# A transformer block's backward pass on one core: another order of work behind the attention

## Chip, core, metric

The kernel runs on one core of a Trainium2 chip, as one program of some 51,000 instructions. The metric is the device time of one execution, in microseconds (us), as the median of several runs. The engines named below are TensorE (PE, matrix products and transposes; PEld is its loading of weights), VectorE (DVE), ScalarE (ACT), GpSimd (POOL) and SyncE (SP, which here only issues DMA transfers). Each engine takes its own instructions in program order and waits for other engines by semaphores. On-chip tiles lie in SBUF; matrix products are summed in banks of PSUM.

## What is computed

The forward value of one block and all gradients of it, for a sequence of 2048 with D = 512, 32 heads of 16 and a hidden width F of 1792, in bfloat16:

```python
xn = layernorm(x)
s  = softmax_attention(xn @ wqkv) @ wo               # A_ref
y  = layernorm(xn)
h  = gelu_tanh(y @ w1 + b1)
g  = silu(h @ w2 + b2)                               # silu of B_ref
out = x + s * g
out, vjp = jax.vjp(f, x, wqkv, wo, w1, b1, w2, b2)
return out, *vjp(grad_out)    # outputs 0..7: out, dx, dwqkv, dwo, dw1, db1, dw2, db2
```

## The kernel before

It has three parts that run one after the other. The first (`phase_pre`, from line 42) computes the projections, the MLP's forward part and the gates, and puts into DRAM what the last part needs: `H1T_s` (the MLP's pre-activation, transposed), `HGT_s` (its gelu, transposed), `GB_s` (per row the gate g and grad_out times a gate factor), `DSO_s` (the gradient at the attention's output projection), `Y_s` (y). The second (`attention_core`, line 822) runs forward and backward of the attention for 16 pairs of heads, with PE, ACT and DVE in orders that are written out by hand. It leaves the attention's output O in the SBUF tile `Oall` and the gradients of q, k and v in `dQall` and DRAM (`dKVT_s`). The diff touches neither.

The third part, `phase3` (line 498), is the post-attention part. The sequence is cut into NT = 16 tiles of 128 rows, D into IC = 4 blocks, F into FC = 14 blocks; `FG` groups the 14 blocks by 4, 4, 4 and 2. PSUM is split into four banks for products over 512 rows or columns (`psA`), two for transposes (`psT`), two for the weight gradients (`psW`). In order:

- Output stage (L556 to L611). For each of 16 row tiles: O is transposed by PE (`o_turn`, `o_tp`, copied by ACT to `oTt`), multiplied with wo (`ps_so`, L595, four matmuls). DVE multiplies the product with one gate to `dm_all` (the gradient dm at the MLP's output) and with the other to `t1`; POOL adds x to `t1` into `ot`, which is stored every fourth tile as out_0 (issued by POOL). `dm_turn` transposes dm into `dmT`. The gates come as `gb4`, 1 MB for four row tiles, by SP (`load4`); w2 comes transposed by a DMA (`w2T`).
- db2 and dwo (L614 to L631): column sums of dm by 16 matmuls with a vector of ones (`psdb2`), then four tiles `ps_dwo` of 16 matmuls from O and `ds4`, each copied by ACT and stored.
- dw2 (L632 to L645): 14 tiles `ps_dw2` of 16 matmuls, from `hgc` (gelu, turned by DMA: one set of four transposes by SP for two tiles) and `dm_all`.
- dh1 and dw1 (L648 to L688). For each of the 14 blocks of F, 4 x 4 matmuls `ps_dhg` of w2T and dmT; DVE multiplies the product with gelu' into `dh1T`, where gelu' lay, and sums it for db1. A DMA transposes each block into `dhc`. When a group of FG is done, the four tiles `ps_dw1` of the group before follow (16 matmuls each, of `y_all` and `dhc`), copied by ACT to one of two buffers `dw1` and stored by POOL. The last group has two blocks, so its matmuls have 256 columns. w1 is loaded transposed (`w1T`) after the second group.
- dy (`ps_dy`, L719), with the backward of the second layer norm on ACT and DVE, then dx, dwq and dwkv. Unchanged.

gelu' is computed between these: `gelu_grad` (L533) does one of 28 pieces (two blocks of F by 512 rows, tiles of 128x1024). It loads `h1` by SP; then ACT Square, DVE L542 and L543 (`w`), ACT Identity and two Sigmoids (the second of the negative), and four steps on DVE (L549 to L552), the last of which writes into dh1T. Two pieces are called in the output stage (after row tiles 11 and 15), one with each dwo tile, one with each dw2 tile, and the rest before the dh1 blocks of the later groups.

The order on each engine in this part is set by the tile scheduler, which emits instructions by the waits it foresees; the program's order is a preference only. Within `tc.manual_schedule(engines=...)` the named engines keep the program's order. Where two tiles share a place in SBUF, the later one waits for the last use of the earlier one. The pools take places from the left or right side of SBUF in the order in which they are opened, and give them back when closed.

Of the kernel before, what the change touches and what calls it, by code (L numbers as in the profile page):

```python
# [8 lines left out]
bf16 = mybir.dt.bfloat16  # L9
f32 = mybir.dt.float32  # L10
# [487 lines left out]
def phase3(ctx, tc, k, A_x, A_wqkv, A_wo, B_w1, B_w2, grad_out, out_0, out_1, out_2, out_3, out_4, out_5, out_6, out_7, dbg):  # L498
# [14 lines left out]
    with ExitStack() as c1:  # L513
# [12 lines left out]
        with ExitStack() as cL:  # L526
# [6 lines left out]

            def gelu_grad(j, g):

                cs = slice(g * 512, (g + 1) * 512)
                h1 = ew.tile([128, 2, 512], bf16, name="h1", bufs=3)
                nc.sync.dma_start(out=h1[:], in_=k.H1T_s[j, g])
                sq = ew.tile([128, 2, 512], bf16, name="sq")
                nc.scalar.activation(out=sq[:], in_=h1[:], func=ACT.Square, scale=float(np.sqrt(2.0 * GC * GA)))  # L540
                w = ew.tile([128, 2, 512], bf16, name="w", bufs=1)
                nc.vector.tensor_scalar(out=w[:], in0=sq[:], scalar1=2.0 * GC, scalar2=None, op0=ALU.add)  # L542
                nc.vector.tensor_tensor(out=w[:], in0=w[:], in1=h1[:], op=ALU.mult)  # L543
                nc.scalar.activation(out=sq[:], in_=sq[:], func=ACT.Identity, scale=3.0, bias=c2gc[:])
                sg = ew.tile([128, 2, 512], bf16, name="sg")
                nc.scalar.activation(out=sg[:], in_=w[:], func=ACT.Sigmoid)
                sp = ew.tile([128, 2, 512], bf16, name="sp")
                nc.scalar.activation(out=sp[:], in_=w[:], func=ACT.Sigmoid, scale=-1.0)
                nc.vector.tensor_tensor(out=sp[:], in0=sp[:], in1=h1[:], op=ALU.mult)  # L549
                nc.vector.tensor_tensor(out=sp[:], in0=sp[:], in1=sq[:], op=ALU.mult)  # L550
                nc.vector.tensor_scalar(out=sp[:], in0=sp[:], scalar1=1.0, scalar2=None, op0=ALU.add)
                nc.vector.tensor_tensor(out=dh1T[:, 2 * j:2 * j + 2, cs], in0=sp[:], in1=sg[:], op=ALU.mult)  # L552
            gel = [(j, g) for j in range(FC // 2) for g in range(4)]

            cM = cL.enter_context(ExitStack())
            dmp = pool(cM, "p3_dm", side="right")  # L556
            dm_all = dmp.tile([128, NT, D], bf16, name="dm_all")
            with ExitStack() as c2:
# [21 lines left out]
                nc.sync.dma_start_transpose(out=w2T[:], in_=B_w2)  # L580
                o_turn(0)
                o_turn(1)

                def dm_turn(t):
# [3 lines left out]
                    nc.scalar.copy(out=dmT[:, :, t * 128:(t + 1) * 128], in_=pt[:])  # L588
                for t in range(NT):
                    if t % 4 == 1 and t + 4 < NT:  # L590
                        load4(t // 4 + 1)
                    ps = psA.tile([128, D], f32, name="ps_so", tag="mm")
                    o = oTt.pop(t)
                    for cc in range(IC):
                        nc.tensor.matmul(ps[:], lhsT=o[:, cc, :], rhs=wo_sb[:, cc, :], start=(cc == 0), stop=(cc == IC - 1))  # L595
                    gb = gb4[t // 4]
                    nc.vector.tensor_tensor(out=dm_all[:, t, :], in0=ps[:], in1=gb[:, t % 4, 1, :], op=ALU.mult)
                    t1 = b2.tile([128, D], f32, name="t13")
                    nc.vector.tensor_tensor(out=t1[:], in0=ps[:], in1=gb[:, t % 4, 0, :], op=ALU.mult)
                    if t % 4 == 0:  # L600
                        ot = b2.tile([128, 4, D], bf16, name="ot3")
                    nc.gpsimd.tensor_tensor(out=ot[:, t % 4, :], in0=t1[:], in1=x4[t // 4][:, t % 4, :], op=ALU.add)
                    if t % 4 == 3:
                        nc.gpsimd.dma_start(out=rows4(o0, t // 4), in_=ot[:])
                    if t + 2 < NT:
                        o_turn(t + 2)
                    if t >= 1:
                        dm_turn(t - 1)
                    if t in (11, 15):
                        gelu_grad(*gel.pop(0))  # L610
                dm_turn(NT - 1)  # L611
            with ExitStack() as c2:
                b2 = pool(c2, "p3a_dw2", 2, side="right")
                ds4 = [b2.tile([128, 4, D], bf16, name="ds4", bufs=4) for q4 in range(4)]  # L614
# [8 lines left out]
                for ac in range(IC):  # L623
# [7 lines left out]
                    gelu_grad(*gel.pop(0))  # L631
                for fc in range(FC):  # L632
                    if fc % 2 == 0:
                        hgc = b2.tile([128, 4, 2, 4, 128], bf16, name="hgc")
                        for g in range(4):
                            nc.sync.dma_start_transpose(out=hgc[:, g].rearrange("p l t f -> p (l t) f"),
                                                        in_=k.HGT_s[fc // 2, g].rearrange("p l c -> p (l c)"))
                    ps = psW.tile([128, D], f32, name="ps_dw2", tag="w")
                    for t in range(NT):
                        nc.tensor.matmul(ps[:], lhsT=hgc[:, t // 4, fc % 2, t % 4, :], rhs=dm_all[:, t, :], start=(t == 0), stop=(t == NT - 1))  # L640
                    dw2 = b2.tile([128, D], bf16, name="dw2")
                    nc.scalar.copy(out=dw2[:], in_=ps[:])
                    nc.gpsimd.dma_start(out=out_6[fc * 128:(fc + 1) * 128, :], in_=dw2[:])
                    gelu_grad(*gel.pop(0))
            cM.close()  # L645
            w1T = pool(cL, "p3_w1").tile([128, FC, D], bf16, name="w1T")
            with ExitStack() as c2:
                b2 = pool(c2, "p3b", 2, side="right")  # L648
                y_all = b2.tile([128, NT, D], bf16, name="y_all", bufs=1)
                nc.sync.dma_start(out=y_all[:].rearrange("p (g t) d -> p g t d", g=4), in_=k.Y_s.rearrange("g p t d -> p g t d"))  # L650
                dhc = {}

                def do_dw1(gi):
                    f0, nf = FG[gi]
                    fn = nf * 128
                    for ic in range(IC):
                        ps = psW.tile([128, 512], f32, name="ps_dw1", tag="w")
                        for t in range(NT):
                            nc.tensor.matmul(ps[:, 0:fn], lhsT=y_all[:, t, ic * 128:(ic + 1) * 128], rhs=dhc[gi][:, t, 0:fn],
                                             start=(t == 0), stop=(t == NT - 1))  # L660
                        dw1 = b2.tile([128, 512], bf16, name="dw1")
                        nc.scalar.copy(out=dw1[:, 0:fn], in_=ps[:, 0:fn])
                        nc.gpsimd.dma_start(out=out_4[ic * 128:(ic + 1) * 128, f0 * 128:f0 * 128 + fn], in_=dw1[:, 0:fn])
                for gi, (f0, nf) in enumerate(FG):
                    dhc[gi] = b2.tile([128, NT, 512], bf16, name="dhc")
                    for fl in range(nf):
                        fc = f0 + fl
                        if gi and gel:
                            gelu_grad(*gel.pop(0))
# [17 lines left out]
                nc.vector.tensor_copy(out=db1[:], in_=db1f[:])  # L687
                nc.sync.dma_start(out=out_5.rearrange("(c p) -> p c", p=128), in_=db1[:])  # L688
            cW.close()

# [613 lines left out]
```

## Time and profile before

| | us |
|---|---|
| median of 3 runs (2321.96 to 2326.19) | 2322.59 |
| profiled execution, of which the span of its instructions | 2325.73, 2324.0 |
| PE busy in the span (96%) | 2228.9 |
| ACT busy (88%) | 2046.3 |
| DVE busy (87%) | 2021.2 |
| POOL busy (15%) | 341.9 |

The columns of the next table are the stretch of the span in us, its length, busy us of PE and of DVE, and the clock that PE was granted as a share of full speed.

| stretch | what runs on PE | length | PE | DVE | clock |
|---|---|---|---|---|---|
| 0 to 155 | first part | 155.0 | 129.98 | 102.39 | 0.97 |
| 155 to 1959 | attention | 1804.0 | 1771.60 | 1697.72 | 1.00 |
| 1959 to 1965 | start of the third part | 6.0 | 1.31 | 3.77 | 0.87 |
| 1965 to 2000.5 | output stage, first dh1 matmuls | 35.5 | 32.15 | 30.64 | 0.97 |
| 2000.5 to 2015.8 | dwo | 15.3 | 14.05 | 10.92 | 1.00 |
| 2015.8 to 2073 | dw2 | 57.2 | 50.85 | 32.67 | 0.97 |
| 2073 to 2098.5 | dh1 | 25.5 | 18.15 | 22.07 | 0.89 |
| 2098.5 to 2171.3 | dh1 and dw1 | 72.8 | 72.35 | 46.71 | 0.99 |
| 2171.3 to 2187.9 | the last of dw1 | 16.6 | 7.72 | 0.00 | 0.69 |
| 2187.9 to 2324 | dy, dx, dwqkv | 136.1 | 130.68 | 74.31 | 0.99 |

Where PE is busy for less than the length of a row, it waits for something there.

### The profile page before, as it was taken

The page shows a single profiled execution, that of the slowest core. Times are in us where ns is not written, and L with a number is a line of the kernel's source. Part 1 is how long each engine was busy: PE and PEld are TensorE (multiplying, and loading weights), DVE is VectorE, ACT ScalarE, POOL GpSimd, SP SyncE. Part 2 cuts the span into 40 slices and gives each one's busy share as a digit, 9 for nine tenths or more (in the row PEclk, how much of TensorE's full clock was granted, in tenths as well). Part 3 has the DMA queues.
Part 4 walks back from the last instruction along what each step waited for, and adds up shares of the span by engine and source line. Part 5 has one row for each costly group of instructions (what it writes and reads, how often), then busy time and mean ns, then how long its engine had stood idle before and what let it go on. Part 6 is the DMA issues. An engine that isn't in the chain of part 4 may idle for free.

```text
span 2324.0 us, 50898 instructions
## 1 busy us (share of the span) xinstructions
PE 2228.9 (96%) x20082; PEld 796.1 (34%) x20128; DVE 2021.2 (87%) x3593; ACT 2046.3 (88%) x2337; POOL 341.9 (15%) x804
## 2 busy tenths in 40 slices
PE   7898999999999999999999999999999998889899
PEld 3342333333333333333333333333333333434444
DVE  6577899999999999999999999999999996767255
ACT  6566999999999999999999999999999999786133
POOL 4330111111111111111111111111111111310000
PEclk9999999999999999999999999999999999999999
DMA  9787999999998999999999999999999898996961
GB/s 287 229 279 176 169 174 169 179 163 184 161 186 163 180 167 179 165 179 168 175 175 167 180 164 186 163 184 162 181 167 179 155 160 195 241 212 138 169 181 65
DMA packets 1310113, 415.56 MB, mean 179 GB/s; under 512 B 1272273, under 2 KB 1285073, under 8 KB 1308721
## 3 DMA queue, kind: packets, MB, share of 16 engines
q1 hardware_dynamic: 1303984, 395.92, 90.3%
q0 software_dynamic: 4304, 12.98, 1.7%
q10 hardware_dynamic: 1584, 3.41, 0.4%
q8 instruction: 157, 2.57, 0.4%
q14 instruction: 84, 0.68, 0.1%
HBM read 46.52 MB, written 49.03 MB: 41 GB/s over the span
## 4 chain that ended last, share of the span: by engine, by line
PE 77%; issue 8%; DVE 8%; DMA 3%; ACT 2%; POOL 1%; SPq 1%; ACTq 0%; POOLq 0%; DVEq 0%
PE d L933 12%; PE X L970 11%; PE s L911 11%; PE Z L1051 9%; PE X L983 7%; PE Z L1043 5%; DVE gts L950 5%; PE t L923 5%; PE ET L895 5%; PE ps_dy L719 2%; PE XT L995 2%; PE X L973 1%; PE ps_dwkv L752 1%; PE ps_dxa L771 1%; DMA out_dram<-dw 1%
## 5 line engine op out<-in xcount | busy, mean ns | idle before, releaser
L950 DVE TENSOR_TENSOR gts<-d,et 128x512 bf16<-128x512 f32 x2048 | 1321.8, 684 | 73.8 <-PE d L933 23.0
L939 ACT ACTIVATE et<-s 128x1024 bf16<-128x1024 f32 x1024 | 1043.0, 1044 | 8.9 <-PE d L933 8.2
L944 ACT ACTIVATE e<-t 128x1024 bf16<-128x1024 f32 x832 | 866.2, 1042 | 25.2 <-PE t L923 5.4
L933 PE MATMUL d<-QDT,KVT 32*128 32x512 bf16 x2048 | 757.2, 384 | 18.2 <-DVE gts L950 16.9
L911 PE MATMUL s<-QDT,KVT 32*128 32x512 bf16 x2048 | 398.5, 385 | 5.0 <-ACT et L939 2.9
L1051 PE MATMUL Z<-gk,W 128*32 128x512 bf16 x2048 | 397.5, 385 | 0.0
L970 PE MATMUL X<-et,Lc 128*32 128x512 bf16 x2048 | 369.8, 389 | 0.0
L973 PE MATMUL X<-et,NAT 128*32 128x512 bf16 x2048 | 368.7, 388 | 0.0
L983 PE MATMUL X<-gts,NAT 128*17 128x512 bf16 x2048 | 330.4, 381 | 0.0
L1043 PE MATMUL Z<-e,W 128*32 128x512 bf16 x1664 | 321.8, 383 | 3.9 <-POOL W L1022 1.6
L923 PE MATMUL t<-KVT,QDT 32*128 32x512 bf16 x1664 | 323.6, 384 | 1.0 <-ACT e L944 1.0
L933 PEld LDWEIGHTS <-KVT 32*128 32x128 bf16 x2048 | 173.1, 91 | 234.8 <-issue 234.4
L911 PEld LDWEIGHTS <-KVT 32*128 32x128 bf16 x2048 | 106.1, 91 | 250.0 <-issue 230.3
L1017 POOL TENSOR_TENSOR W<-NATQd,rL 128x128 bf16<-128x128 bf16 x64 | 25.8, 403 | 1124.2 <-DVE rL L1016 1124.1
L1051 PEld LDWEIGHTS <-W 128*32 128x32 bf16 x2048 | 100.3, 95 | 172.9 <-issue 142.8
L923 PEld LDWEIGHTS <-QDT 32*128 32x128 bf16 x1664 | 92.3, 91 | 145.8 <-issue 141.0
L1043 PEld LDWEIGHTS <-W 128*32 128x32 bf16 x2048 | 105.0, 94 | 107.4 <-issue 96.7
L970 PEld LDWEIGHTS <-Lc 128*32 128x32 bf16 x2048 | 83.5, 93 | 162.2 <-issue 162.1
L900 DVE COPY eE<-ET 128x1024 bf16<-128x1024 bf16 x192 | 130.2, 678 | 4.4 <-PE ET L895 4.4
L895 PE MATMUL ET<-ident_bf,et 128*128 128x128 bf16 x1536 | 119.2, 220 | 2.1 <-DVE e L286 2.1
L895 PEld LDWEIGHTS <-et 128*128 128x128 bf16 x1536 | 86.5, 98 | 45.8 <-issue 45.8
L983 PEld LDWEIGHTS <-NAT 128*17 128x17 bf16 x2048 | 79.5, 89 | 59.4 <-issue 42.8
(203 smaller groups left out, 2354.1 us busy)
## 6 DMA issues: line engine op xcount, KB each, us to landing
gk<-gts SPq DMA_TRANSPOSE x512, 4.5
H1T_s<-h1p SPq DMA_DIRECT2D x28, 256.0 KB, 4.3
h<-H1T_s SPq DMA_DIRECT2D x28, 256.0 KB, 3.6
HGT_s<-hgT SPq DMA_DIRECT2D x21, 256.0 KB, 4.3
NAT_s<-NS SPq DMA_DIRECT2D x4, 1056.0 KB, 5.4
dKVT_s<-ob SPq DMA_DIRECT2D x16, 256.0 KB, 3.7
gb<-GB_s SPq DMA_DIRECT2D x4, 1024.0 KB, 6.8
Rkv<-dKVT_s SPq DMA_DIRECT2D x2, 2048.0 KB, 9.4
```

Source lines behind the costliest of these rows:

```text
L895: nc.tensor.transpose(ET[:, hj, m * 128:(m + 1) * 128], st_et[g - 3 + m][:, hj, 384:512], ident_bf[:])
L911: nc.tensor.matmul(s[:, hj, :], lhsT=op["KVT"][r, kb * 128:(kb + 1) * 128], rhs=op["QDT"][r, qc * 512:(qc + 1) * 512], start=True, stop=Tr ...
L923: nc.tensor.matmul(t[:, hj, :], lhsT=op["QDT"][r, q0:q0 + 128], rhs=op["KVT"][r, kc * 512:(kc + 1) * 512], start=True, stop=True, tile_pos ...
L933: nc.tensor.matmul(d[:], lhsT=op["KVT"][r, kb * 128:(kb + 1) * 128], rhs=op["QDT"][r, qc * 512:(qc + 1) * 512], start=True, stop=True, til ...
L939: nc.scalar.activation(out=et[:], in_=st_s.pop(g)[:], func=ACT.Exp)
L944: nc.scalar.activation(out=e[:], in_=st_t.pop(g)[:], func=ACT.Exp)
L950: nc.vector.tensor_tensor(out=gts[:, g % 2, hj], in0=st_d.pop((g, hj))[:], in1=st_et[g][:, hj], op=ALU.mult)
L970: nc.tensor.matmul(X[64 + 32 * hj:96 + 32 * hj, :], lhsT=Lc[:, :], rhs=et[:, hj, :], start=(kb == 0), stop=False, skip_group_check=True, t ...
L973: nc.tensor.matmul(X[32 * hj:32 * hj + 32, :], lhsT=NATt[:, kb, hj, 1:33], rhs=et[:, hj, :], start=(kb == 0), stop=(kb == 15), tile_positi ...
L983: nc.tensor.matmul(X[64 + 32 * hj:64 + 32 * hj + 17, :], lhsT=NATt[:, kb, hj, 0:17], rhs=gts[:, kb % 2, hj, :], start=False, stop=(kb == 1 ...
L1043: nc.tensor.matmul(Z[32 * hj:32 * hj + 32, :], lhsT=blk[j]["W1"][:, qb, hj, :], rhs=e[:, hj, :], start=(qb == 0), stop=False, tile_positio ...
L1051: nc.tensor.matmul(cur["Z"][32 * hj:32 * hj + 32, :], lhsT=blk[j]["W2"][:, qb, hj, :], rhs=grhs, start=False, stop=(qb == 3), tile_positio ...
```

## The change

All of it lies in `phase3`. gelu' is cut into three functions: `gelu_a` (load, Square, two DVE steps), `gelu_b` (Identity and the two Sigmoids, the one of the negative now first) and `gelu_c` (four DVE steps). The output stage keeps the program's order on PE, ACT and DVE; three pieces of gelu' are laid into it by these parts, where two whole ones were before. `t13` has three buffers for two. `dm_all` moves to the left side. The dw2 tile becomes a function; tiles 0 to 9 come as before, tiles 10 to 13 each before one of the first four dh1 blocks, and each of these four blocks now takes a piece of gelu' as well. `y_all` takes O's place (`Oall`) in place of a tile of its own. The pool of w1T is opened after the first dh1 group, and the odd `dhc` go to a pool of their own on the left. `dw1` has eight buffers for two.

```diff
--- before.py
+++ after.py
@@ -531,9 +531,10 @@
             cW = cL.enter_context(ExitStack())
             ew = pool(cW, "p3_ew", 2, side="right")
 
-            def gelu_grad(j, g):
-
-                cs = slice(g * 512, (g + 1) * 512)
+            gu = {}
+
+            def gelu_a(j, g):
+
                 h1 = ew.tile([128, 2, 512], bf16, name="h1", bufs=3)
                 nc.sync.dma_start(out=h1[:], in_=k.H1T_s[j, g])
                 sq = ew.tile([128, 2, 512], bf16, name="sq")
@@ -541,19 +542,32 @@
                 w = ew.tile([128, 2, 512], bf16, name="w", bufs=1)
                 nc.vector.tensor_scalar(out=w[:], in0=sq[:], scalar1=2.0 * GC, scalar2=None, op0=ALU.add)
                 nc.vector.tensor_tensor(out=w[:], in0=w[:], in1=h1[:], op=ALU.mult)
+                gu[j, g] = h1, sq, w
+
+            def gelu_b(j, g):
+                h1, sq, w = gu[j, g]
                 nc.scalar.activation(out=sq[:], in_=sq[:], func=ACT.Identity, scale=3.0, bias=c2gc[:])
                 sg = ew.tile([128, 2, 512], bf16, name="sg")
-                nc.scalar.activation(out=sg[:], in_=w[:], func=ACT.Sigmoid)
                 sp = ew.tile([128, 2, 512], bf16, name="sp")
                 nc.scalar.activation(out=sp[:], in_=w[:], func=ACT.Sigmoid, scale=-1.0)
+                nc.scalar.activation(out=sg[:], in_=w[:], func=ACT.Sigmoid)
+                gu[j, g] = h1, sq, sg, sp
+
+            def gelu_c(j, g):
+                h1, sq, sg, sp = gu.pop((j, g))
                 nc.vector.tensor_tensor(out=sp[:], in0=sp[:], in1=h1[:], op=ALU.mult)
                 nc.vector.tensor_tensor(out=sp[:], in0=sp[:], in1=sq[:], op=ALU.mult)
                 nc.vector.tensor_scalar(out=sp[:], in0=sp[:], scalar1=1.0, scalar2=None, op0=ALU.add)
-                nc.vector.tensor_tensor(out=dh1T[:, 2 * j:2 * j + 2, cs], in0=sp[:], in1=sg[:], op=ALU.mult)
+                nc.vector.tensor_tensor(out=dh1T[:, 2 * j:2 * j + 2, g * 512:(g + 1) * 512], in0=sp[:], in1=sg[:], op=ALU.mult)
+
+            def gelu_grad(j, g):
+                gelu_a(j, g)
+                gelu_b(j, g)
+                gelu_c(j, g)
             gel = [(j, g) for j in range(FC // 2) for g in range(4)]
 
             cM = cL.enter_context(ExitStack())
-            dmp = pool(cM, "p3_dm", side="right")
+            dmp = pool(cM, "p3_dm")
             dm_all = dmp.tile([128, NT, D], bf16, name="dm_all")
             with ExitStack() as c2:
                 b2 = pool(c2, "p3a", 2, side="right")
@@ -578,39 +592,63 @@
                     nc.scalar.copy(out=oTt[t][:], in_=pt[:])
                 load4(0)
                 nc.sync.dma_start_transpose(out=w2T[:], in_=B_w2)
-                o_turn(0)
-                o_turn(1)
 
                 def dm_turn(t):
                     pt = psT.tile([128, IC, 128], bf16, name="dm_tp", tag="tp")
                     for b in range(IC):
                         nc.tensor.transpose(pt[:, b, :], dm_all[:, t, b * 128:(b + 1) * 128], k.ident_bf[:])
                     nc.scalar.copy(out=dmT[:, :, t * 128:(t + 1) * 128], in_=pt[:])
-                for t in range(NT):
-                    if t % 4 == 1 and t + 4 < NT:
-                        load4(t // 4 + 1)
+                ot = {}
+
+                def so(t):
                     ps = psA.tile([128, D], f32, name="ps_so", tag="mm")
                     o = oTt.pop(t)
                     for cc in range(IC):
                         nc.tensor.matmul(ps[:], lhsT=o[:, cc, :], rhs=wo_sb[:, cc, :], start=(cc == 0), stop=(cc == IC - 1))
                     gb = gb4[t // 4]
                     nc.vector.tensor_tensor(out=dm_all[:, t, :], in0=ps[:], in1=gb[:, t % 4, 1, :], op=ALU.mult)
-                    t1 = b2.tile([128, D], f32, name="t13")
+                    t1 = b2.tile([128, D], f32, name="t13", bufs=3)
                     nc.vector.tensor_tensor(out=t1[:], in0=ps[:], in1=gb[:, t % 4, 0, :], op=ALU.mult)
                     if t % 4 == 0:
-                        ot = b2.tile([128, 4, D], bf16, name="ot3")
-                    nc.gpsimd.tensor_tensor(out=ot[:, t % 4, :], in0=t1[:], in1=x4[t // 4][:, t % 4, :], op=ALU.add)
+                        ot[t // 4] = b2.tile([128, 4, D], bf16, name="ot3")
+                    nc.gpsimd.tensor_tensor(out=ot[t // 4][:, t % 4, :], in0=t1[:], in1=x4[t // 4][:, t % 4, :], op=ALU.add)
                     if t % 4 == 3:
-                        nc.gpsimd.dma_start(out=rows4(o0, t // 4), in_=ot[:])
-                    if t + 2 < NT:
-                        o_turn(t + 2)
-                    if t >= 1:
-                        dm_turn(t - 1)
-                    if t in (11, 15):
-                        gelu_grad(*gel.pop(0))
-                dm_turn(NT - 1)
+                        nc.gpsimd.dma_start(out=rows4(o0, t // 4), in_=ot[t // 4][:])
+                with tc.manual_schedule(engines={mybir.EngineType.PE, mybir.EngineType.Activation, mybir.EngineType.DVE}):
+                    o_turn(0)
+                    o_turn(1)
+                    for t in range(NT):
+                        if t % 4 == 1 and t + 4 < NT:
+                            load4(t // 4 + 1)
+                        so(t)
+                        if t + 2 < NT:
+                            o_turn(t + 2)
+                        if t >= 1:
+                            dm_turn(t - 1)
+                        if t in (4, 8, 12):
+                            gelu_a(*gel[0])
+                        if t in (5, 9, 13):
+                            gelu_b(*gel[0])
+                        if t in (6, 10, 14):
+                            gelu_c(*gel.pop(0))
+                    dm_turn(NT - 1)
+            hgp = pool(cM, "p3_hg", 2)
+
+            def do_dw2(fc):
+                if fc % 2 == 0:
+                    hgc[fc // 2] = hgp.tile([128, 4, 2, 4, 128], bf16, name="hgc")
+                    for g in range(4):
+                        nc.sync.dma_start_transpose(out=hgc[fc // 2][:, g].rearrange("p l t f -> p (l t) f"),
+                                                    in_=k.HGT_s[fc // 2, g].rearrange("p l c -> p (l c)"))
+                ps = psW.tile([128, D], f32, name="ps_dw2", tag="w")
+                for t in range(NT):
+                    nc.tensor.matmul(ps[:], lhsT=hgc[fc // 2][:, t // 4, fc % 2, t % 4, :], rhs=dm_all[:, t, :], start=(t == 0), stop=(t == NT - 1))
+                dw2 = hgp.tile([128, D], bf16, name="dw2")
+                nc.scalar.copy(out=dw2[:], in_=ps[:])
+                nc.gpsimd.dma_start(out=out_6[fc * 128:(fc + 1) * 128, :], in_=dw2[:])
+            hgc = {}
             with ExitStack() as c2:
-                b2 = pool(c2, "p3a_dw2", 2, side="right")
+                b2 = pool(c2, "p3a_dwo", 2, side="right")
                 ds4 = [b2.tile([128, 4, D], bf16, name="ds4", bufs=4) for q4 in range(4)]
                 for q4 in range(4):
                     nc.sync.dma_start(out=ds4[q4][:], in_=k.DSO_s[q4])
@@ -629,26 +667,15 @@
                     nc.scalar.copy(out=dwo[:], in_=ps[:])
                     nc.gpsimd.dma_start(out=out_3[ac * 128:(ac + 1) * 128, :], in_=dwo[:])
                     gelu_grad(*gel.pop(0))
-                for fc in range(FC):
-                    if fc % 2 == 0:
-                        hgc = b2.tile([128, 4, 2, 4, 128], bf16, name="hgc")
-                        for g in range(4):
-                            nc.sync.dma_start_transpose(out=hgc[:, g].rearrange("p l t f -> p (l t) f"),
-                                                        in_=k.HGT_s[fc // 2, g].rearrange("p l c -> p (l c)"))
-                    ps = psW.tile([128, D], f32, name="ps_dw2", tag="w")
-                    for t in range(NT):
-                        nc.tensor.matmul(ps[:], lhsT=hgc[:, t // 4, fc % 2, t % 4, :], rhs=dm_all[:, t, :], start=(t == 0), stop=(t == NT - 1))
-                    dw2 = b2.tile([128, D], bf16, name="dw2")
-                    nc.scalar.copy(out=dw2[:], in_=ps[:])
-                    nc.gpsimd.dma_start(out=out_6[fc * 128:(fc + 1) * 128, :], in_=dw2[:])
-                    gelu_grad(*gel.pop(0))
-            cM.close()
-            w1T = pool(cL, "p3_w1").tile([128, FC, D], bf16, name="w1T")
+            for fc in range(10):
+                do_dw2(fc)
+                gelu_grad(*gel.pop(0))
             with ExitStack() as c2:
-                b2 = pool(c2, "p3b", 2, side="right")
-                y_all = b2.tile([128, NT, D], bf16, name="y_all", bufs=1)
+                b2 = pool(c2, "p3b", 1, side="right")
+                y_all = k.Oall
                 nc.sync.dma_start(out=y_all[:].rearrange("p (g t) d -> p g t d", g=4), in_=k.Y_s.rearrange("g p t d -> p g t d"))
                 dhc = {}
+                cD = cL.enter_context(ExitStack())
 
                 def do_dw1(gi):
                     f0, nf = FG[gi]
@@ -658,14 +685,21 @@
                         for t in range(NT):
                             nc.tensor.matmul(ps[:, 0:fn], lhsT=y_all[:, t, ic * 128:(ic + 1) * 128], rhs=dhc[gi][:, t, 0:fn],
                                              start=(t == 0), stop=(t == NT - 1))
-                        dw1 = b2.tile([128, 512], bf16, name="dw1")
+                        dw1 = b2.tile([128, 512], bf16, name="dw1", bufs=8)
                         nc.scalar.copy(out=dw1[:, 0:fn], in_=ps[:, 0:fn])
                         nc.gpsimd.dma_start(out=out_4[ic * 128:(ic + 1) * 128, f0 * 128:f0 * 128 + fn], in_=dw1[:, 0:fn])
                 for gi, (f0, nf) in enumerate(FG):
-                    dhc[gi] = b2.tile([128, NT, 512], bf16, name="dhc")
+                    if gi == 1:
+                        cM.close()
+                        w1p = pool(cL, "p3_w1")
+                        dhc1 = pool(cD, "p3_dhc1")
+                        w1T = w1p.tile([128, FC, D], bf16, name="w1T")
+                    dhc[gi] = (dhc1 if gi % 2 else b2).tile([128, NT, 512], bf16, name="dhc")
                     for fl in range(nf):
                         fc = f0 + fl
-                        if gi and gel:
+                        if not gi:
+                            do_dw2(10 + fl)
+                        if gel:
                             gelu_grad(*gel.pop(0))
                         for sc in range(4):
                             ss = slice(sc * 512, (sc + 1) * 512)
@@ -686,6 +720,7 @@
                 db1 = b2.tile([128, FC], bf16, name="db1", bufs=1)
                 nc.vector.tensor_copy(out=db1[:], in_=db1f[:])
                 nc.sync.dma_start(out=out_5.rearrange("(c p) -> p c", p=128), in_=db1[:])
+            cD.close()
             cW.close()
 
             cR = c1.enter_context(ExitStack())
```

## Prediction

> **What bounds the kernel now.** First I read the share of the engines in 40 slices: TensorE (PE) is at 9 tenths nearly throughout, and the first slices below that are the ones behind the attention, which ends about 1959 us; everything the change touches lies behind it. So I cut the rest into stretches at the points where PE passes from one kind of matmul to the next. The columns are the stretch, its length, busy us of PE, weight loads, VectorE (DVE), ScalarE (ACT) and GpSimd (POOL) with instruction counts, PE's granted clock, DMA share, GB/s:
>
> ```profile
> 1959.00:1965.00 6.00, 1.31 (x9) 0.95 (x10) 3.77 (x7) 4.98 (x7) 0.00 (x0) 0.87 0.65 203
> 1970.00:1994.70 24.70, 22.08 (x173) 11.95 (x176) 22.19 (x36) 18.29 (x32) 20.25 (x19) 1.00 0.67 237
> 2015.80:2073.00 57.20, 50.85 (x222) 21.83 (x225) 32.67 (x60) 48.09 (x55) 7.55 (x14) 0.97 1.08 215
> 2073.00:2098.50 25.50, 18.15 (x65) 6.78 (x66) 22.07 (x55) 17.42 (x20) 1.07 (x2) 0.89 0.90 216
> 2111.30:2171.30 60.00, 59.60 (x280) 27.70 (x284) 34.21 (x88) 24.39 (x29) 5.40 (x10) 1.00 0.70 111
> 2171.30:2180.20 8.90, 0.02 (x1) 0.02 (x1) 0.00 (x0) 0.66 (x2) 0.00 (x0) 0.71 1.23 122
> 2180.20:2187.90 7.70, 7.70 (x49) 5.95 (x49) 0.00 (x0) 1.03 (x3) 2.15 (x4) 0.67 0.45 109
> ```
>
> The row at 2171.3 is an empty PE. In the output stage (1970 to 1994.7) DVE is as busy as PE. Then the waits of 1940 to 2190 (us in total, times, longest):
>
> ```profile
> POOL out_dram L663 <- ACT dw L662: 104.7, 15, 34.4
> ...
> DVE sp L549 <- ACT sp L548: 32.6, 15, 4.3
> ...
> ACT sq L544 <- DVE w L542: 17.0, 20, 1.7
> ...
> ACT dw L662 <- DMA out_dram<-dw: 12.8, 1, 12.8
> ...
> PE ps_dw L659 <- ACT dw L662: 8.9, 1, 8.9
> ...
> PE ps_dhg L674 <- DVE db1p L676: 7.1, 9, 2.0
> ...
> PE o_tp L577 <- ACT oTt L578: 4.5, 1, 4.5
> ```
>
> One wait of 8.9 us is on a dw1 copy, which itself waits for a store to free one of two buffers (the chain of waits has that store: issued 2163.59, landed 15.85 us later). Around gelu', ACT and DVE wait for each other. Last, the time line of DVE and POOL where gelu' meets the output adds:
>
> ```profile
> 1986.47 0.95 DVE L552 TENSOR_TENSOR dh1T<-sp,sg 128x1024 bf16<-128x1024 bf16 x1
> ...
> 1993.24 0.95 DVE L549 TENSOR_TENSOR sp<-sp,h 128x1024 bf16<-128x1024 bf16 x1
> 1994.12 1.37 DVE L542 TENSOR_SCALAR w<-sq 128x1024 bf16<-128x1024 bf16 x1
> 1995.41 0.68 DVE L550 TENSOR_TENSOR sp<-sp,sq 128x1024 bf16<-128x1024 bf16 x1
> ```
>
> POOL adds from 1983.49 to 1988.4 and from 1990.26 to 1995.2. Under it gelu' operations take 0.95 and 1.37 us; behind it 0.68, and 0.42 for L542 elsewhere.
>
> **The ledger before.** A 512-column matmul costs 0.216 us (16 of ps_dwq in 3.45). From the last attention matmul (1958.97) to the first ps_dy (2187.88) PE has 784 of them, 64 of 256 columns (0.108 each) and 120 transposes (0.055, from four per 0.22): 182.5 us of work in 228.9. The 46.4 us of stall are: start, to the first ps_so at 1964.76, 5.4; output stage and 27 early dh1 matmuls, to dwo at 2000.56, 6.5 (35.8 less 29.3); dwo 1.4; dw2 8.9; dh1 up to the first dw1 at 2098.47, 11.5 (25.5 less 65 x 0.216); on to 2171.29, 3.0; the empty 8.9; 0.8 because the 64 after it take 7.7 where 6.9 would do. Now each under the change, by the two programs' instruction orders.
>
> **Eight dw1 buffers.** A copy now waits for the store eight copies earlier. The copies at 2179.5 would wait for stores issued by 2149.8 that landed in 2.0. The 8.9 goes, and with it the slow clock: -9.7. What is late next? ps_dy needs w1T, loaded long before, and the layer-norm behind it y rows, whose load waits for this same PE point. If that load sits behind the dQT transposes it may be 4 us late, under four ps_dy banks of 3.0 us each. So nothing is added.
>
> **Start: +0.4.** No o_tp is left to do here; PE idles 5.8 until wo_sb lands, whose place in SP's queue (behind the dKVT store of 1959.73) is unchanged.
>
> **Output stage, laid out.** The gate load (gb4, 1 MB) now sits where the attention's ob lay: it waits for the dKVT store, which lands 3.1 after 1959.73. It is issued about 1963.0 rather than 1961.0. Gate loads landed in 5.1 to 8.6, the first in 6.2; I take 5.6, as wo_sb is nearly through. The first dm multiply can start at 1968.6 (before: 1970.0, behind gelu'). From there DVE has, up to dm of tile 15: 31 multiplies at 0.60 = 18.6; three halves a (0.60 + 0.34) = 2.8; three halves c (3 x 0.60 + 0.34) = 6.4; one more L542 and one dh1 step, 1.0. That is 28.8. Before, two gelu' and a half ran on idle engines ahead of the stage; here all three run in it. The order is fixed, so DVE also waits for ACT: c0 for copy, Identity 1.05, table load 1.28 and sigmoid 0.95 (about 1.1), a1 1.1, a2 0.6, small ones 0.8: 3.6. Slower gelu' operations under POOL are not shown for this order. Bounds: 0 (POOL's add trails DVE's t1 and is often over when c begins) and 9.0 (all 12 wide ones +0.27, all 6 narrow ones +0.95); I take 1.0, since the a halves meet an add and the c halves mostly don't. Then 7.6 until enough dh1 banks are free for PE to reach dwo: five steps at 0.61 and eight gelu' or t1 operations. Together 41, so dwo at 2009.6. PE does ten more dh1 matmuls by then: 31.9 of work in 44.8, stall 12.9 rather than 6.5: +6.4. The cost is DVE's; PE and ACT (about 28 of these 41) lie beside it.
>
> The Trainium skill (SBUF — State Buffer, Who interferes with whom) says of such pairs that the shared port is an exclusive lock and "the loser fully blocks". If each of the 18 operations had to wait half of a 1.19 us add, this would be an estimated 10.7 instead of my 1.0 and the change would lose; the rows at 1993 to 1995 agree that there is a toll.
>
> **A new wait: db2.** Its tile now lies on the second ot buffer, so ACT's db2 copy waits for the last output store. Queued behind it on ACT are gelu' number 4 and the dwo copies; the second dwo tile needs db2's bank. Store: issued about 2004.6, landing 7.6 (the four took 6.9, 8.3, 2.9, 9.6), so db2 at 2012.8, where PE has waited since 2010.5: 2.3. Then seven ACT operations of about 0.98 stand before the first dwo copy, 2020.4, while PE is out of banks at 2018.8: 1.6. Stall 3.9 instead of 1.4: +2.5.
>
> **dw2, dh1 in between, y, w1T.** w1T leaves the head of the third hgc set (9.12 us of SP, then PE waits of 3.16 and 0.73): -3.9. In its place y (2 MB) is loaded once dwo is done, beside hgc, and two dhc transposes (1.96 each in the median) stand ahead of the fourth set; of these 3.9 I charge 2.7, as a set has about a microsecond of slack. dw2 then stalls 7.7. The last two dw2 tiles lie among only eleven dh1 tiles' matmuls. Then PE has 40 dh1 matmuls (8.6) to the first dw1, which needs the fourth dhc; that is queued behind w1T, which waits for the last dw2 since it takes dm_all's place: 9.12 + 0.5 + 1.96 + 4.5 to land = 16.1, stall 7.5. Bounds: 3 if w1T goes at w2T's 7.04 and h1 is early, 10 if it lands like the dhc beside y (12.1). 15.2 instead of 20.4: -5.2.
>
> **Sigmoids exchanged.** With 1-s first, DVE's product runs under the other sigmoid: ACT's round of 5.14 us (sigmoids 2074.19 to 2079.33) falls to its own work, 3.9 + 0.47 = 4.4. I count it at nothing: it covers the later start of the chain (number 16 at 2068 instead of 2077, PE there about 2075). Without it some 4 us would be lost.
>
> **Sum:** 0.4 + 6.4 + 2.5 - 5.2 - 9.7 = -5.6. The profiled execution took 2325.73 (span 2324.0) and would take 2320.1; it is 3.1 above the median of the runs, 2322.59, so the forecast is **2317.0**.
>
> **Rivals.**
> A, larger gain: DVE and ACT mesh without waits (-3.6), the last store lands in 2.9 (-2.5 of waiting), w1T by its lower bound (-4.5, less the few that DVE then binds, say -1.5 net): 2309.4. For it: ACT has slack in the stage. Against: the table load now sits inside it.
> B, slower: DVE and POOL collide as a rule. Place: the stage. Price: 9.0 instead of 1.0, and POOL's store issued later still and landing in 9.6, +2.0: +4.4 net, 2327.0. It turns the sign from 6.6 us of collisions on. For: the three rows above. Against: POOL's adds follow DVE's t1 and mostly end before the next c.
> C, the removed wait returns: 8.9 us of PE idleness stay before ps_dy because the dQT transposes and stores still share a DMA at 1.23 busy: 2317.0 + 8.9 = 2325.9, not distinguishable from no change. Against: no matmul there reads dQT.
> D, gains and losses cancel within the bounds: 2322.
>
> **How the numbers follow.** A measurement of this kernel can tell 0.2%, 4.6 us. Chances: forecast 0.42 (own range 2313 to 2321, 0.27 of it beyond 0.2%), A 0.27, B 0.15, C 0.06, D 0.10. Faster 0.54, same 0.28 (0.12 of the forecast, C, D), slower 0.18 (B and the rest). The range reaches from A less 4 more (the sigmoid exchange, counted at nothing, shortening the chain) to B: 2305 to 2327.
>
> **What would show it.** Right: no PE wait on dw1 copies, and 64 half matmuls near 6.9; first dm at 1968 to 1969; last dm near 2002; PE waiting once for db2; dw1 beginning some 16 us behind the last dw2 with w1T between. Wrong: last dm before 1997 (A) or after 2006 (B), or a PE gap of 5 us or more before ps_dy (C).

## The result and the profile after

The changed kernel takes 2327.09 us (median of 20 runs, 2324.38 to 2330.48), the kernel before 2323.38 (20 runs, 2318.94 to 2328.14). The ratio is 1.0015, with a 95% interval of 1.0008 to 1.0021: slower by 1.9 to 4.9 us. Forecast was 2317.0, with a range of 2305 to 2327. The profiled execution took 2326.7, its span is 2324.9.

The stretches of the profile after, cut where PE passes to the next kind of matmul; the columns are those of the prediction's first fence (stretch, length, busy us of PE, PEld, DVE, ACT and POOL with counts, granted clock, DMA share, GB/s):

```profile
1957.74:1963.52 5.78, 0.00 (x0) 0.02 (x1) 0.68 (x1) 0.00 (x0) 0.00 (x0) 0.73 0.67 164
1963.52:2014.68 51.16, 39.25 (x237) 18.70 (x237) 43.90 (x72) 37.37 (x52) 22.55 (x21) 0.93 0.58 205
2028.83:2089.89 61.06, 53.97 (x237) 22.87 (x236) 38.19 (x71) 50.58 (x59) 7.59 (x14) 0.97 1.01 228
2089.89:2107.83 17.94, 10.73 (x41) 4.11 (x40) 15.06 (x37) 13.21 (x15) 0.54 (x1) 0.89 1.02 213
2107.83:2187.49 79.66, 79.39 (x392) 38.63 (x393) 44.32 (x114) 32.48 (x40) 8.12 (x15) 0.98 0.75 106
```

The last row has no hole: the empty 8.9 us in front of dy are gone. The second row, the output stage up to dwo, is 51.16 us long where it was 35.80, and DVE is busy for 43.90 of them.

With each matmul at 0.216 us, 256-column ones at 0.108 and transposes at 0.055, as in the prediction's ledger, the stall of PE in each stretch (length less work, us) is:

| stretch | before | predicted | after |
|---|---|---|---|
| start, to the first ps_so | 5.4 | 5.8 | 5.8 |
| output stage, to dwo | 6.5 | 12.9 | 19.3 |
| dwo | 1.4 | 3.9 | 0.3 |
| dw2 and dh1, to the first dw1 | 20.3 | 15.2 | 19.6 |
| dw1, to the first dy | 12.5 | 3.0 | 1.9 |
| dy to the last matmul (its length) | 131.4 | 131.4 | 132.8 |

So the profile after is longer by 0.8 of stall and 1.4 at the end; the attention ended 1.24 us earlier in it (1957.74 for 1958.98), which makes the 0.97 us by which the two profiled executions differ. The medians differ by 3.7, since the profiled execution before was 2.35 us above the median of its 20 runs, the one after 0.39 below.

The waits of 1940 to 2190 in the profile after (us in total, times, longest):

```profile
POOL ot L614 <- DVE t L611: 39.0, 7, 22.4
...
DVE sp L558 <- ACT sp L552: 29.9, 20, 2.7
...
PEld L599 <- DVE dm_all L609: 9.4, 7, 2.1
...
PE dm_tp L599 <- DVE dm_all L609: 7.1, 7, 2.0
...
PE ps_dw L645 <- DMA hgc<-HGT_s: 4.8, 5, 2.9
...
PE ps_dw L686 <- DMA dhc<-dh1T: 3.5, 1, 3.5
...
ACT dw L647 <- DMA out_dram<-dw: 2.1, 1, 2.1
```

No PE wait on a dw1 copy is left. The largest of PE's waits in the stage is for DVE's dm. Why DVE is late shows in its own time line (start, length, line, operation):

```profile
1967.27 0.69 DVE L609 TENSOR_TENSOR dm_all<-ps_so,gb 128x512 bf16<-128x512 f32 x1 [8.81 <-DMA gb<-GB_s]
...
1985.31 0.43 DVE L543 TENSOR_SCALAR w<-sq 128x1024 bf16<-128x1024 bf16 x1 [0.27 <-ACT sq L541]
1985.77 1.93 DVE L544 TENSOR_TENSOR w<-w,h 128x1024 bf16<-128x1024 bf16 x1
1987.63 0.68 DVE L609 TENSOR_TENSOR dm_all<-ps_so,gb 128x512 bf16<-128x512 f32 x1
...
1990.73 1.53 DVE L559 TENSOR_TENSOR sp<-sp,sq 128x1024 bf16<-128x1024 bf16 x1
...
2004.94 0.68 DVE L609 TENSOR_TENSOR dm_all<-ps_so,gb 128x512 bf16<-128x512 f32 x1
```

The first and the last of these lines are the first and the last dm. POOL's time line around 1985:

```profile
1983.92 1.16 POOL L614 TENSOR_TENSOR ot<-t,x 128x512 bf16<-128x512 f32 x1 [3.79 <-DVE t L611]
1985.38 0.57 POOL L616 DMA_DIRECT2D out_dram<-ot  x1 [0.30 <-POOL ot L614]
1985.98 1.17 POOL L614 TENSOR_TENSOR ot<-t,x 128x512 bf16<-128x512 f32 x1
```

POOL's add runs to 1987.15; L544 ends 0.55 us behind it, about the 0.6 that it needs alone: it lay there for the whole add. Six steps of the three pieces are stretched: L543 once to 1.43 (0.43 alone), L558 once to 1.32, L544 twice to 1.93 and L559 twice to 1.53 (0.69 alone): 1.01 + 0.64 + 2 x 1.24 + 2 x 0.84 = 5.8 us.

### The profile page after: what moved, and what is told of

It is laid out like the page before. It is cut to its first block, busy times and chain, and to the rows that moved or that the text cites. A ratio compares the mean times of both kernels' runs of the same rounds, so it can differ in the third digit from the quotient of the medians.

```text
span 2324.9 us, 50918 instructions
## 1 busy us (share of the span) xinstructions
PE 2230.2 (96%) x20128; PEld 794.9 (34%) x20128; DVE 2028.5 (87%) x3593; ACT 2046.2 (88%) x2337; POOL 342.7 (15%) x804
## 6 DMA issues: line engine op xcount, KB each, us to landing
Rkv<-dKVT_s SPq DMA_DIRECT2D x2, 2048.0 KB, 10.3
```

## The experiments

In all of them the ratio stands against runs of the kernel before on the same chip. "Stage" is the stretch from the first ps_so to dwo.

**Eight buffers alone.** Before, with the one line (eight do not fit there):

```diff
-                        dw1 = b2.tile([128, 512], bf16, name="dw1")
+                        dw1 = b2.tile([128, 512], bf16, name="dw1", bufs=6)
```

> The kernel before with six dw1 buffers in place of two, and nothing else changed (eight do not fit beside its own y tile). Theory S (the profiled waits are the cost in every execution, the loss of the change lies in the output stage): the 8.9 us of an empty PE behind the dw1 matmuls go and nothing takes their place, some 2314.5 us against 2323.4. Rival R (the profile of before was 2.4 us above its median, so its 15.85 us store was an unlucky one and the wait is mostly short): 2319 to 2323. Rival T (the wait comes back later, in front of dy or behind it): 2322 to 2324, with a new PE gap behind 2171.

2309.64 us, ratio 0.9950 (0.9938 to 0.9963), the lowest of all kernels here. From the first dw1 to dy the profile shows, with columns as above:

```profile
2090.66:2168.14 77.48, 77.07 (x388) 38.01 (x389) 46.77 (x118) 35.39 (x42) 7.54 (x14) 1.00 0.76 113
```

77.48 us where it was 89.41: -11.9, and the clock at 1.00. Rivals R and T fall.

**Two buffers in the changed kernel** (`bufs=8` to `bufs=2`).

> The changed kernel with two dw1 buffers again. Theory S: the wait for the store returns, 8 to 10 us on top of 2327.1, about 2336. Rival R: 2328 to 2331. Rival T: within 1 us of 2327.1.

2338.20, ratio 1.0076 (1.0063 to 1.0088). The stretch from dw1 to dy is 94.10 us for 79.66. The waits in it (us in total, times, longest):

```profile
ACT dw L689 <- DMA out_dram<-dw: 14.3, 1, 14.3
...
PE ps_dw L686 <- ACT dw L689: 10.5, 1, 10.5
```

So the buffers bring 12 us in the kernel before and some 14 in the changed one, and the rest of the change costs 15 to 18 (1.0015 for 0.9950 with the buffers, 1.0076 for 1 without them).

**The adds cut**, first and again. POOL adds only 8 of 512 columns, into two `ot` tiles that it sets to zero ahead of the stage; for the other columns x + s*g is left out.

```diff
...
-                    nc.gpsimd.tensor_tensor(out=ot[t // 4][:, t % 4, :], in0=t1[:], in1=x4[t // 4][:, t % 4, :], op=ALU.add)
+                    nc.gpsimd.tensor_tensor(out=ot[t // 4][:, t % 4, 0:8], in0=t1[:, 0:8], in1=x4[t // 4][:, t % 4, 0:8], op=ALU.add)
```

> The changed kernel with POOL's adds of the output stage cut to 8 of 512 columns, in two buffers that POOL zeroes once ahead of the stage; the sum x + s*g is left out for the other columns. All waits, stores and orders stay. Theory S (the gelu' steps of DVE are stretched by POOL's adds: 1.01 + 0.64 + 1.24 + 0.84 + 1.24 + 0.84 = 5.8 us in the profile): the stretched steps of 1.32 to 1.93 us fall to 0.42 and 0.69, the last dm multiply comes 5 to 6 us earlier, about 2321.5 us. Rival O (the stage is long because of its fixed order and ACT's sigmoids in it, the long DVE steps lie beside other waits): less than 1.5 us of gain, 2325.5 to 2327.

> The changed kernel with POOL's adds cut to 8 of 512 columns (x + s*g is left out for the others), once more. Theory S: 4 to 6 us below the changed kernel on the same chip. Rival O: within 2 us of it, although the steps of 1.32 to 1.93 us are at 0.43 and 0.69 in the profile.

> The changed kernel unchanged, on the same chip as the three others, as their measure: about 0.15% over the kernel before. Its profile shows whether the stage's 51 us from the first ps_so to dwo, and the collisions in it, are the same in another execution (a fixed order: within 1 us), and how far the end of the attention varies (1954.97 to 1961.98 us in the profiles so far).

First 2323.98, ratio 1.0013 (1.0004 to 1.0022), no clear step from the changed kernel's 1.0015. Beside the changed kernel on one chip: 2323.24, ratio 1.0000 (0.9991 to 1.0009), for 2330.21, ratio 1.0025 (1.0015 to 1.0035): 7.0 us. In the profiles the stage is 46.00 and 47.24 us with the cut, 51.16 and 51.91 without. The second pair's stage, without and with the cut (columns as above):

```profile
1964.47:2016.38 51.91, 37.59 (x238) 17.93 (x238) 43.87 (x72) 36.75 (x51) 22.37 (x21) 0.96 0.58 201
1961.12:2008.36 47.24, 38.14 (x236) 18.64 (x236) 38.95 (x74) 38.19 (x53) 7.41 (x21) 0.93 0.64 220
```

The same steps in DVE's time line of the first run with the cut, each at its own length:

```profile
1982.84 0.43 DVE L543 TENSOR_SCALAR w<-sq 128x1024 bf16<-128x1024 bf16 x1 [1.08 <-ACT sq L541]
1983.30 0.69 DVE L544 TENSOR_TENSOR w<-w,h 128x1024 bf16<-128x1024 bf16 x1
...
1987.02 0.69 DVE L559 TENSOR_TENSOR sp<-sp,sq 128x1024 bf16<-128x1024 bf16 x1
```

In the second profile of the changed kernel the stretched steps are the same, to 0.02 us: the order is fixed, and so is what meets in it. In the stage theory S holds: the stretched steps cost it 4.7 to 5.2 us. In the whole time it holds in the second pair (7.0 us) and not in the first (some 0.5 us by the two ratios, which stand against different runs of the kernel before). What the stage gains need not reach the end: in the second pair's profiles the first dw1 comes 149.66 us behind the attention's end with the cut and 148.82 without.

**gelu' ahead of the stage**, without and with the adds cut.

```diff
+                for _ in range(3):
+                    gelu_grad(*gel.pop(0))
                 with tc.manual_schedule(engines={mybir.EngineType.PE, mybir.EngineType.Activation, mybir.EngineType.DVE}):
...
-                        if t in (4, 8, 12):
-                            gelu_a(*gel[0])
...
```

> The changed kernel with the three pieces of gelu' called in front of the output stage, which keeps its fixed order, in place of within it. Theory S: DVE has two or three pieces less to do in the stage and no wide step beside POOL's adds except those the scheduler spreads; the last dm multiply some 8 us earlier, about 2319 us. Rival O (the fixed order itself costs): at most 2 us gained, 2325 to 2327, with DVE and PE still waiting for ACT's copies in the stage.

> The changed kernel with the three pieces of gelu' called ahead of the laid-out stage (2320.3 us by itself, where five DVE steps still took 1.04 to 2.51 us beside POOL's adds, 5.4 us more than alone) and, besides, POOL's adds cut to 8 of 512 columns; the sum x + s*g is left out for the others. Theory S (collisions are real time): the stage from the first ps_so to dwo falls from 40.9 to about 35.5 us, as long as that of before, so the laid-out order itself costs nothing; the time falls by some 5 us to 2315. Rival O (what is lost is the order, collisions only fill waits): the stage stays above 39 us and the time within 1.5 us of 2320. That a whole run shows less than its profile, as with the cut adds and gelu' in the stage (profile -5.2 us in the stage, median -1), is left to be told by this pair.

2320.25, ratio 0.9996 (0.9987 to 1.0004); and 2315.65, ratio 0.9966 (0.9952 to 0.9979). The stage is 40.93 and 37.65 us with 30 dh1 matmuls in it, so its stall is 10.5 and 7.3, for 6.5 before. The two ratios are 7 us apart, their stages 3.3: theory S's time, and a stage between the two theories. In the first the scheduler put the next piece between the multiplies, and DVE's time line again has a step that waits for two adds:

```profile
1978.82 2.51 DVE L544 TENSOR_TENSOR w<-w,h 128x1024 bf16<-128x1024 bf16 x1
```

With neither gelu' nor whole adds in it, the laid-out order has 0.8 us more of stall than the stage of before, which has its adds: it is mainly what is in the order that costs.

**The old stage in the changed kernel, and the new one in the kernel before.** The blocks were exchanged whole (the second with six dw1 buffers and the exchanged sigmoids).

> The changed kernel with the output stage of before (its order left to the scheduler, two whole pieces of gelu' called after tiles 11 and 15); eight dw1 buffers, dw2 tiles between dh1 tiles, y in O's place and the exchanged sigmoids stay. Theory S (the laid-out stage costs some 13 us, the eight buffers bring 12, the rest about nothing): 2311 to 2315 us where before is 2322 to 2323. Rival M (the rest, that is the new order of dw2, dh1, y and w1T, costs as much as the stage): 2318 to 2321. Rival N (all the loss is in the rest): 2324 to 2327.

> The kernel before with six dw1 buffers (2309.6 us by itself) and the new output stage: laid-out order, three pieces of gelu' in it, sigmoids exchanged; dw2, dh1, y and w1T as before. Theory S: the stage adds 12 to 15 us, 2321 to 2325. Rival M: it adds 6 to 8, 2316 to 2318. Rival N: 2309 to 2312.

2316.27, ratio 0.9970 (0.9960 to 0.9979), and 2328.71, ratio 1.0029 (1.0018 to 1.0039). The new stage costs 0.45% (10.5 us) in the one setting and 0.79% (18.3 us) in the other. Theory S is the nearest in both, but each time lies outside what it gave, 1.3 us above 2315 and 3.7 above 2325. The stage is 35.09 and 51.08 us long. What makes the two costs differ is not shown. In the profiles the difference lies in dwo: with the old stage dwo comes early, and the wait that the prediction named appears, in the waits of 2000 to 2022 of the first run:

```profile
ACT db L650 <- DMA out_dram<-ot: 6.1, 1, 6.1
PE ps_dwo L655 <- ACT db L650: 2.7, 1, 2.7
```

dwo takes 19.42 us there and 14.15 in the changed kernel; in the other setting it takes 13.81 with the new stage and 14.86 with six buffers alone. The next run shows that db2 is only a part of it.

**db2's tile apart**, on the version with y rows from O's place (next): `db2 = base.tile(...)` for `b2.tile(...)`.

> The changed kernel with the old output stage and y rows from O's place (2313.1 us), and the db2 tile in a pool that shares no place with the stage's ot buffers. Theory S (ACT's db2 copy waited 6.0 us for the last output store there, PE 2.6 and 0.9 for dwo banks): the stretch from the first dwo to the first dw2 falls from 19.3 to about 15 us, the time to some 2309. Rival N (dwo then waits for ds4, whose two last loads wait for the same stores, or the gelu' pieces ahead of the dwo copies decide): 2312 to 2313.

2314.23, ratio 0.9965 (0.9953 to 0.9978), against 0.9967: no gain that can be told. dwo fell from 19.29 to 16.83 us, less far than theory S had it, since PE now waits 2.18 us for ds4 there, as rival N said. The first dw1 came 139.0 us behind the attention's end, for 139.6, so most of the 2.5 us were not left by then.

**y rows from O's place**, in the kernel before with y there and eight buffers, and in the changed kernel with the old stage.

```diff
-                        nc.sync.dma_start(out=y4[q4][:], in_=k.Y_s[q4])
...
-                    tmp, nms = ln_bwd_tail(nc, wk, z[:], y4[t // 4][:, t % 4, :], s1[:], rs)
+                    tmp, nms = ln_bwd_tail(nc, wk, z[:], k.Oall[:, t, :], s1[:], rs)
```

> The kernel before with eight dw1 buffers, y loaded into O's place, and the layer-norm's y rows read from there in place of four loads of 512 KB; stage and order as before. Theory S (these parts only take waits away): 2305 to 2310 us, at or a little below the 2309.6 of six buffers, and DVE's wait for y at the start of dy is gone. Rival N (y in O's place delays the hgc or dhc transposes behind its 2 MB): 2312 to 2316.

> As the changed kernel with the old output stage, and the layer-norm's y rows read from O's place, without the four loads behind dw1. Theory S: 1 to 2 us below the same without it, since the changed kernel's dx matmuls waited 1.3 us in all behind late y rows. Rival N: no difference (under 0.5 us in the profile from the first dy to the end).

2313.68, ratio 0.9967 (0.9955 to 0.9979), and 2313.12, ratio 0.9967 (0.9955 to 0.9979). The first is in rival N's range: 4 us above the six buffers, though the intervals overlap. It has 83.0 us from dw2 to dw1 where six buffers had 78.8; that y's 2 MB now stand among the hgc loads is a likely reason, not one that was tried, and two executions of the changed kernel differ by 3.1 us in this stretch (79.00 and 75.93). The second run's program also names the w1T load one group later, but SP issues it at the same place, behind the second dhc transpose. It is right in the profile (dy to the last matmul 131.39 us for 132.63), within the interval in the median. In the changed kernel DVE's time line has a wait for y at dy's start:

```profile
2199.48 0.69 DVE L488 CUSTOM_DVE_ANT_0 lnb_prod<-lnb_z,y 128x512 f32<-128x512 f32 x1 [7.82 <-DMA y<-Y_s]
```

**The sigmoids**, back in the changed kernel, and exchanged in the kernel before with six buffers.

> The changed kernel with the two sigmoids of a gelu' piece in their order before. The prediction held that the exchange shortens the round of ACT and DVE from 5.14 to 4.4 us and covers 4 us of a later start. Theory X (that holds): the first dw1 comes 3 to 5 us later, about 2331 us. Rival Y (the rounds are bound by other work): within 1.5 us of 2327.

> The kernel before with six dw1 buffers (2309.6 us) and the sigmoids exchanged, all else as before. Theory X: the rounds of 5.14 us between dw2's end and the first dw1 fall to some 4.4 us, of which four or five lie there: the stretch from the end of dw2 to the first dw1 falls from 23.2 to about 20 us, 2306 to 2307 us. Rival Y: 2309 to 2310.

2325.34, ratio 1.0017 (1.0008 to 1.0025) for 1.0015, and 2310.96, ratio 0.9954 (0.9942 to 0.9965) for 0.9950: rival Y twice. The stretch from the end of dw2 to the first dw1 did fall in the second, from 23.2 to 19.6 us, but dw2 in front of it was 5.2 us longer (60.8 for 55.6).

**Two w buffers**, in the kernel before with four dw1 buffers, and in the changed kernel (`name="w", bufs=2`).

> The kernel before with four dw1 buffers and two buffers for gelu's w (one before); six dw1 buffers alone gave 2309.6 us. Theory C (the chain of gelu' pieces, ACT and DVE taking turns through one w, sets when dw1 begins: 5.14 us a round with 3.9 us of ACT's work in it): with two w the rounds shorten by up to 1.2 us, the 12 us of PE idleness between dw2's end and the first dw1 fall to under 5, some 2302 us. Rival D (dw1's start is set by the transposes of hgc, h1 and dhc on SP's queue): 2309 to 2311, the stretch from dw2's end to the first dw1 stays near 23 us. Should four dw1 buffers be too few, an idle PE behind 2150 shows it.

> The changed kernel with two buffers for w. Theory C: the stretch from the first dw2 to the first dw1 (79.0 us) falls by 4 to 8 us; the output stage stays long, some 2320 us. Rival D: within 1.5 us of 2327.

2324.24, ratio 1.0000 (0.9991 to 1.0009), and 2328.63, ratio 1.0022 (1.0012 to 1.0032) for 1.0025 on that chip. Theory C falls in the second. The first says little of it: four dw1 buffers are too few (PE waits 4.16 us for a copy at 2183, the copies 7.6 for stores).

## Why the prediction failed, by its own steps

- **Eight buffers, -9.7: right, too small.** -11.9 by itself. With the wait goes also most of the 3.0 us that the ledger had left standing in front of it: from 12.5, the stall falls to 0.6 with six buffers and to 1.9 after (-10.6).
- **Output stage, +6.4: the step that failed.** It was +12.8 (19.3 for 6.5), and +13.5 in the second profile (51.91 us less 31.9 of work, for 6.5). The stage ended in B's sign: the last dm came 47.20 us behind the attention's end, where 43.0 was forecast and the mark of B, 2006, is 47.0. From the first dm to the last it took 37.67 us (37.65 in the second profile) for 33.4, and 33.50 and 33.95 with the adds cut. Two terms were too small, the first above all.
  - Collisions of DVE and POOL: taken as 1.0 with bounds of 0 and 9.0, because POOL's adds "trail DVE's t1 and are often over when c begins". Measured 5.8, of which the cut gave back 5.2 and 4.7 in the stage. An add starts behind each t1 and lasts 1.17 us, and in the fixed order each half a or c stands right behind a t1, so the first of its steps or the second meets an add each time. The rows of 0.95 and 1.37 us that spoke for it were cited and then set aside. Rival B had mechanism and place right, but held that 6.6 us turn the sign; with the other terms as they came, 5.8 were enough.
  - From the last dm to dwo: 9.74 us (10.07 in the second profile) for 7.6, with PE waiting 1.29 for dh1 banks and 0.93 for ds4, a wait that no term had.
  - The other terms of gelu' in the stage were nearly right: without the adds, 33.50 and 33.95 us from the first dm to the last, where 32.4 remain of the forecast. What the three pieces themselves cost shows where they are called ahead: with the adds cut, the stage's stall is 14.6 (15.8 in the repeat) with them in it and 7.3 without.
- **The first dm at 1968.6:** 9.53 us behind the attention's end, forecast 9.63. Right.
- **db2, +2.5: the wait is real, hidden here.** The stage became so late that the store was nearly there (dwo stalls 0.3). With the old stage dwo stalls 5.6, of which 2.5 went with db2's tile apart.
- **dw2, dh1, y, w1T, -5.2: wrong.** -0.7 here (19.6 for 20.3), and 16.5 in the second profile after, 16.4 with six buffers and the old order: no gain beyond the spread. dw2 stalls 10.3 where 7.7 were forecast. Its waits for hgc are 4.8 us, for 5.2 before: w1T no longer stands ahead of the third set, but two dhc transposes stand ahead of the fourth (5.65 us of SP), and there PE waits 2.89 and 0.74, nearly what it had waited behind w1T (3.16 and 0.73). Behind dw2 the 40 matmuls were there as said, but the stall is 9.3 for 7.5 (dw1 begins 17.9 us behind the last dw2, 16.1 forecast): PE waited 1.69 and 2.06 for DVE's dh1 steps and 3.45 for dhc, with its clock at 0.89.
- **Sigmoids at nothing: right; that they cover 4 us: wrong.** Without the exchange nothing is lost in the time.
- **Nothing added behind dy: wrong by 1.4.** The y rows came late, as said, and DVE waited 7.8 us, but the work that piled up held ACT's copies, and with them three dx matmul groups.
- **The ground:** 3.1 us were taken off for the profiled execution's distance from three runs; against 20 runs it was 2.35.

The terms beside the stage came to -10.6, and -12.0 was forecast. That they are so near is luck: the db2 wait that did not show (3.6 less than forecast) makes up for most of the gain in dw2 and dh1 that did not come (4.5).

Rival A fell with the stage, C (the wait comes back before dy) with the 79.66 and 77.48 us from dw1 to dy, and D holds in part: some 11 us of gain were cancelled by a loss nearly all of which is in one stage.

The Trainium skill (SBUF — State Buffer, Who interferes with whom) says that the later of the two engines waits for the whole instruction of the other. This case's trace agrees on the whole instruction: L544 at 1985.77 ended 0.55 us behind the add. On which of the two is the later it does not plainly agree: by the profile's starts both stretched L544 began 0.2 us ahead of the add (the one shown at 1985.77, its add at 1985.98), while POOL was issuing a store, and waited all the same. By that rule the prediction had an estimate of 10.7 for half an add on each of 18 steps; what it missed both ways is that 6 of 18 meet one, and then nearly all of it (5.8 / 6 = 0.97 of 1.17 us).

What stays open: what sets the first dw1, where 2.5 us gained at dwo did not show. In the changed kernel a second w does not bring it forward, nor does the order of the sigmoids change it; the loads on SP's queue were not tried by themselves. Open is also why the new stage costs 10.5 us in one setting and 18.3 in the other, and why the cut adds brought 0.5 us in one comparison and 7.0 in the next.

## What to carry to other kernels

An order that fixes where two engines meet repeats a collision with every round; where a stage's pace is set by one engine, first count which of its steps fall into the other's instruction, and charge nearly the whole of that instruction to each (0.97 of 1.17 us here). Take a change of several parts apart before keeping it: one line (more buffers for a store that can land 15.85 us late) was worth 12 us, and the rest spent it. A new wait that costs nothing behind a late stage is still there: with the old stage the db2 wait showed with 6.1 us, though taking it away brought no time that could be told.

## What the runs showed of the hardware

- DVE's steps of 128x1024 in bf16, both inputs in SBUF or one, were held up by POOL's adds (0.69 to 1.53, 1.93 and 2.51 us; 0.43 to 1.43), while the multiplies that read PSUM and one SBUF tile stayed at 0.68 and 0.69 beside the same adds.
- The attention, untouched, ended between 1954.97 and 1961.98 us in the 18 profiles, so that one profile says nothing of a few us in the total; the fixed stage repeated within 0.8 us (51.16 and 51.91).
